# A chunk attention and ELU feed-forward kernel on one Trainium2 core: the head crossing moves from v's load into the scores, and sixteen warm-up products stand in place of thirteen

## The chip, the cores and the metric

The kernel runs on one core of one Trainium2 chip. The metric is the device time of one execution in microseconds; the kernel before takes 837.71 us (median of three, 837.11 to 837.82). The engines are TensorE (PE, with its weight loads as PEld), VectorE (DVE), ScalarE (ACT), GpSimd (POOL) and SyncE (SP). SP computes nothing here; it issues nearly all DMA requests.

## The reference

Chunked attention over 8 batches, 8 heads, 576 tokens and 64 columns a head, with chunks of 64 tokens that attend only to themselves, and then a feed-forward layer over the 4608 rows that result (512 columns):

```python
scores = scale * np.matmul(q_c, k_c.transpose(0, 1, 2, 4, 3))
scores = scores - np.max(scores, axis=-1, keepdims=True)
attn = np.exp(scores)
attn = attn / (np.sum(attn, axis=-1, keepdims=True) + 1e-09)
out = np.matmul(attn, v_c)
...
h = x @ w_in                     # 512 -> 2048; x is out with its heads side by side
g = np.where(h > 0.0, h, alpha * (np.exp(np.minimum(h, 0.0)) - 1.0))
return (g @ w_out).astype(np.float32)
```

`w_in` and `w_out` are double precision inputs of 512x2048 and 2048x512. All results are float32.

## The kernel before

**Work.** The 4608 rows are nine blocks of 512 tokens; a block is four tiles of 128 tokens, and a tile is two chunks. For every block the kernel computes `h` in 16 pieces of 128 hidden columns (`hidden`, PE products named `h`), the ELU of each piece (`elu`), and adds its product with `w_out` onto four output tiles (`second_next`, PE products named `o`). Each float32 operand is split into a high and a low part, and every product is three matmuls (`three`, L447). The last six blocks use a scheme with fewer multiplications whose operands are prepared during the earlier blocks; the change does not touch it.

**Weights.** They arrive as 64-bit words. A unit `u` (seventeen, 0 to 16) is one 128-column piece of `w_in` and the 128-row piece of `w_out` of the piece before, loaded by two requests of 512 KB into one of three staging buffers `st` (`load_unit`, L113 and L120). ACT rescales the high words (L134) and converts the low ones (L139); DVE clips (L156) and joins them in two steps (L163, L167); ACT rounds the result to the high part (L171) and DVE subtracts to get the low part (L177). A unit's buffer is free for the unit three later when its L167 is done.

**Attention of the first eight tiles** (`early_attention`). PE turns q and k (in the start with products of 64 columns, L288; later with transposes, L292), ACT copies them out of PSUM (L301 or L299), PE makes the scores (`score`, L263), DVE takes the maximum (L309), ACT the exponentials (L319, for most of the tiles head by head), DVE the normalisation (L332 to L334), PE turns the result (L339), ACT copies it (L344), PE multiplies with v (`multiply_v_crossed`, L255), and ACT copies the result into x (L438 or L433). Tiles 0 to 3 run in the opening part, called the start here; tiles 4 to 7 run inside the first feed-forward block, among its products. All later tiles use the class `Later`, with its own scores and its own product with v (L271), which read an uncrossed v.

**The crossing.** Scores go to two PSUM banks and two halves of the partitions. Before the change, for the second chunk the bank was swapped with the head's parity, so that after the turn (L339) the rows of a chunk's even and odd heads lie in opposite halves of the partitions for the two chunks. The rows of v must then lie in the matching halves, and `load_v_crossed` puts them there with four requests a tile, each 64 tokens of four heads (64 KB, L246).

**The order of the work** is written out by hand: strings of items name each step, and each engine executes its own instructions in the order of these strings. `START` holds the opening part (`w13` is thirteen transposes of the identity at L863, `q0` a load, a digit one step of that tile's attention, `u1` a unit's load, `r` and `d` one step of the weight preparation on ACT and on DVE, `g02` two filler products), `FIRST_BLOCK` the first block. The SP queue is in program order as well. Its requests signal over eight counters in turn, so a request also waits until the request eight before it (of SP and ACT together) has landed.

Of the kernel before, what the change touches and what calls it, by code (L numbers as in the profile page):

```python
# [21 lines left out]
def kernel(  # L22
# [27 lines left out]
    C = 64  # L50
# [186 lines left out]
    halves = [slice(i * C, (i + 1) * C) for i in range(2)]  # L237
    quarters = [(0, 0), (1, 1), (0, 1), (1, 0)]

    def load_v_crossed(n0: int, pool):  # L240

        dst = pool.tile([P, H, D], F32, name="v_sb").rearrange("p (c h) d -> p c h d", c=2)
        for c in range(2):
            b, s0 = divmod(n0 + c * C, S)
            for r in range(2):
                nc.sync.dma_start(  # L246
                    out=dst[halves[r], c],
                    in_=v[b, r ^ c::2, s0:s0 + C, :].rearrange("h t d -> t h d"))
        return dst

    def multiply_v_crossed(x_ps, v_sb, aT):
        for hp in range(NK):
            for c, j in quarters:
                rows = halves[j ^ c]
                nc.tensor.matmul(  # L255
                    x_ps[halves[j], c, hp, :], lhsT=v_sb[rows, c, hp, :],
                    rhs=aT[rows, hp, halves[c]], start=True, stop=True,
                )

    def score(scores, qT, kT, crossed=0):  # L260
        for hp in range(NK):
            for j, c in quarters:
                nc.tensor.matmul(  # L263
                    scores[halves[c], j ^ (c & crossed), hp, :], lhsT=qT[halves[j], hp, halves[c]],
                    rhs=kT[halves[j], hp, halves[c]], start=True, stop=True,
                )

# [11 lines left out]
    def early_attention(tt: int, q_sb, k_sb, get_v, kT, at, a_pool, get_banks, put, by_head: bool,  # L279
                        by_pair=None):  # L280


        both = get_banks()
        for i, src in enumerate((q_sb, k_sb)):
            for n in range(NK):
                if by_pair is not None:
                    for j, half in enumerate(halves):
                        nc.tensor.matmul(  # L288
                            both[half, i, n * P:(n + 1) * P], lhsT=src[:, j, n * D:(n + 1) * D], rhs=by_pair,
                            start=True, stop=True)  # L290
                else:
                    nc.tensor.transpose(  # L292
                        out=both[:, i, n * P:(n + 1) * P], in_=src[:, 2 * n:2 * n + 2, :],
                        identity=ident)
        yield
        qT = at.tile([P, NK, P], F32, name="qT")
        for i, to in enumerate((qT, kT)):
            if by_pair is None:
                nc.scalar.copy(out=to, in_=both[:, i, :].rearrange("p (h t) -> p h t", h=NK))  # L299
            else:  # L300
                nc.scalar.copy(  # L301
                    out=to.rearrange("p h (t u) -> p (h t) u", u=4),
                    in_=both[:, i, :].rearrange("p (u h) -> p h u", u=4))
        yield
        scores = first_halves(both)
        score(scores, qT, kT, 1)
        yield
        mx = sm.tile([P, 2, NK, 1], F32, name="mx")
        nc.vector.tensor_reduce(out=mx, in_=scores, axis=AX.X, op=ALU.max)  # L309
        a = a_pool.tile([P, H, C], F32, name="a")  # L310
        a_heads = a.rearrange("p (h j) t -> p j h t", j=2)
        z = sm.tile([P, 2, NK, 1], F32, name="z")
        if by_head:

            nc.vector.tensor_scalar_mul(mx, mx, -SCALE)
            yield
            for j in range(2):
                for h in range(NK):
                    nc.scalar.activation(  # L319
                        out=a_heads[:, j, h, :], in_=scores[:, j, h, :], func=AF.Exp, scale=SCALE,  # L320
                        bias=mx[:, j, h, :], accum_out=z[:, j, h, :],
                    )
            yield
        else:
            nc.vector.tensor_tensor(
                out=a_heads, in0=scores, in1=mx.broadcast_to([P, 2, NK, C]), op=ALU.subtract
            )
            yield
            nc.scalar.activation(out=a, in_=a, func=AF.Exp, scale=SCALE)
            yield  # L330
            nc.vector.tensor_reduce(out=z, in_=a_heads, axis=AX.X, op=ALU.add)
        nc.vector.tensor_scalar_add(z, z, 1e-9)  # L332
        nc.vector.reciprocal(z, z)
        nc.vector.tensor_tensor(  # L334
            out=a_heads, in0=a_heads, in1=z.broadcast_to([P, 2, NK, C]), op=ALU.mult
        )
        yield
        for hp in range(NK):
            nc.tensor.transpose(  # L339
                out=both[:, 0, hp * P:(hp + 1) * P], in_=a[:, 2 * hp:2 * hp + 2, :],  # L340
                identity=ident)
        yield
        aT = at.tile([P, NK, P], F32, name="qT")
        nc.scalar.copy(out=aT, in_=both[:, 0, :].rearrange("p (h t) -> p h t", h=NK))  # L344
        yield
        x_ps = first_halves(both)
        multiply_v_crossed(x_ps, get_v(), aT)
        yield
        put(tt, x_ps)
        yield  # L350
# [507 lines left out]
    def warm(n: int):  # L858
# [7 lines left out]

    BY_HEAD = (1, 3, 4, 5, 6, 7)
    START = (
        "q0 w13 k0 q1 k1 0 1 u0 0 q2 0 1 q3 r 1 r k2 0 2 1 d 0 0 d 1 1 k3 2 u1 3 3 g02 2 r d 3 u2 "
        "1 2 3 2 d v0 v1 0 g03 r v2 1 0 2 d v3 1 g21 3 2 2 r d 0 3 2 g32 d u3 s 3 0 3 s 2 1 3 g01 "  # L870
        "3 r d r"
    )
# [93 lines left out]
    with (  # L966
# [24 lines left out]
        for item in START.split():  # L991
            kind, n = item[0], item[1:]
            if kind == "w":
                warm(int(n))
            elif kind == "u":
                load_unit(int(n))
            elif kind in "qkv":
                src = {"q": q, "k": k, "v": v}[kind], f"{kind}_sb", int(n) * P, start
                loaded[kind, int(n)] = load_v_crossed(
                    int(n) * P, start) if kind == "v" else load_quads(  # L1000
                    *src, nc.scalar if item in ("k0", "k1") else nc.sync)
            elif kind == "r":
                next(preparation)
            elif kind == "d":
                next(merging)
            elif kind == "s":
                subtract_next()
            elif kind == "g":
                for _ in range(int(n[1:])):
                    nc.tensor.matmul(  # L1010
                        start_ps[int(n[0])][:, 1, NK * C:], lhsT=ident, rhs=two_idents,
                        start=True, stop=True)
            else:
                start_step(item)
# [20 lines left out]
    def early_tile(n: int):  # L1035

        n0 = n * P
        q_sb, k_sb = [load_heads(src, name, n0, io) for src, name in ((q, "q_sb"), (k, "k_sb"))]
        v_sb = load_v_crossed(n0, vio)
        return early_attention(  # L1040
            n % NTT, q_sb, k_sb, lambda: v_sb, k_turned, at, wi1,
            lambda: ps_early.tile([P, 2, DM], F32, name="ps_a"),
# [293 lines left out]
```

## Time and profile before

| | |
|---|---|
| median of three runs | 837.71 us |
| profiled execution, its own time | 838.7 us |
| its span, first to last instruction | 836.9 us |
| PE busy in it | 819.9 us (98%) |
| DVE, ACT, POOL busy | 620.4, 492.8, 186.7 us |
| mean granted TensorE clock | 0.998 |
| moved by DMA | 181.40 MB, mean 217 GB/s |
| v loads of L246 | 32 requests of 64 KB |

Times in the profile are microseconds from the start of the span. A row of the timeline gives start, duration, engine (SPq is SP's queue of instructions), line, operation, and in brackets how long the engine had been idle before and what ended that. A row of the windows view gives, for one stretch, the busy time and count of each engine, then the granted TensorE clock, the share of the DMA engines' time and GB/s. A matmul of float32 operands counts as two instructions in the profile (the 16 products of a tile with v are x32). Tile numbers are left out of the names; u3's request is the fourth L113 row, and so on.

### The profile page before, as it was taken

Reading aid. Unit: us, or ns where it says so; the run is one execution under the profiler, and the core shown is the slowest. Engines: PE = TensorE matmul, PEld = TensorE weight load, DVE = VectorE, ACT = ScalarE, POOL = GpSimd, SP = SyncE. Lnnn points to the kernel's source line nnn. Section 1 sums busy time; section 2 is a strip of 40 time slices with the busy share of each in tenths; the row PEclk is TensorE's granted clock in tenths of the full one; section 3 lists DMA queues with packets and bytes.
Section 4 is the critical chain, followed back from the end, with each engine's and each line's share of the span. In section 5 each row is a group of like instructions: output and inputs, shape, how many; then the busy total and the mean of one; then the engine's idle time right before and its main releaser. Section 6 shows DMA issues by size and latency. Waiting matters only on the chain.

```text
span 836.9 us, 15651 instructions
## 1 busy us (share of the span) xinstructions
PE 819.9 (98%) x5791; PEld 669.5 (80%) x5791; DVE 620.4 (74%) x945; ACT 492.8 (59%) x884; POOL 186.7 (22%) x196
## 2 busy tenths in 40 slices
PE   8879999999999999999999999999999999999997
PEld 7758777888888878788888888888888888888886
DVE  4978987777887688777877765877877547777744
ACT  5888996444554445666566435666556346776541
POOL 0000004444411211134323553324335000000000
PEclk9999999999999999999999999999999999999999
DMA  8756785788499997689999857699966457664666
GB/s 252 180 193 204 234 264 137 212 240 238 140 295 243 273 277 224 204 222 278 259 262 272 218 141 240 178 300 281 268 184 190 132 164 215 195 194 136 186 198 149
DMA packets 212379, 181.40 MB, mean 217 GB/s; under 512 B 74064, under 2 KB 190800, under 8 KB 212304
## 3 DMA queue, kind: packets, MB, share of 16 engines
q1 hardware_dynamic: 209648, 179.62, 76.6%
q10 hardware_dynamic: 2656, 0.79, 0.4%
q8 instruction: 46, 0.75, 0.4%
q14 instruction: 29, 0.24, 0.1%
HBM read 140.51 MB, written 42.99 MB: 219 GB/s over the span
## 4 chain that ended last, share of the span: by engine, by line
PE 84%; DVE 4%; ACT 4%; DMA 3%; issue 2%; SPq 2%; POOL 0%; DVEq 0%; ACTq 0%; POOLq 0%
PE o L447 42%; PE h L447 37%; PE ps_a L263 2%; DMA st<-in_moe_w_out_dram 2%; PE ps_a L271 2%; ACT a L319 1%; PE ps_a L288 1%; SPq L246 1%; PE h L464 1%; ACT st L134 1%; ACT st L139 1%; DMA q_sb<-in_q_dram 1%; SPq L198 0%; DMA wi_hi<-a_dram 0%; DVE xf L163 0%
## 5 line engine op out<-in xcount | busy, mean ns | idle before, releaser
L447 PE MATMUL o<-wo_hi,ghi 128*128 128x512 f32 x352 | 139.4, 396 | 0.0
L447 PE MATMUL o<-wo_hi,glo 128*128 128x512 f32 x352 | 138.2, 393 | 0.7 <-DVE glo L482 0.4
L447 PE MATMUL o<-wo_lo,ghi 128*128 128x512 f32 x352 | 137.9, 392 | 0.3 <-DVE wo_lo L177 0.3
L447 PE MATMUL h<-xhi,wi_hi 128*128 128x512 f32 x324 | 108.3, 395 | 1.4 <-ACT wi_hi L171 1.2
L447 PE MATMUL h<-xlo,wi_hi 128*128 128x512 f32 x324 | 106.8, 390 | 0.0
L703 POOL TENSOR_TENSOR glo<-e,ghi 128x512 fp32r<-128x512 f32 x32 | 41.3, 1291 | 172.8 <-ACT ghi L701 166.3
L447 PEld LDWEIGHTS o<-wo_hi,glo 128*128 128x128 f32 x352 | 66.5, 189 | 15.8 <-DVE glo L482 1.2
L447 PEld LDWEIGHTS o<-wo_hi,ghi 128*128 128x128 f32 x352 | 66.5, 189 | 14.1
L447 PEld LDWEIGHTS o<-wo_lo,ghi 128*128 128x128 f32 x352 | 66.5, 189 | 14.1 <-DVE wo_lo L177 0.6
L447 PE MATMUL h<-wi_lo,wi_hi 128*128 128x512 f32 x288 | 75.0, 396 | 0.0
L768 ACT COPY kept<-h 128x512 f32<-128x512 f32 x72 | 42.1, 585 | 55.4 <-PE h L447 55.4
L447 PEld LDWEIGHTS h<-xhi,wi_hi 128*128 128x128 f32 x324 | 60.6, 188 | 15.4 <-ACT wi_hi L171 1.6
L447 PE MATMUL h<-wo_lo,wi_hi 128*128 128x512 f32 x288 | 71.8, 389 | 0.0
L447 PE MATMUL o<-wo_hi,wo_lo 128*128 128x512 f32 x240 | 71.0, 390 | 0.0
L447 PEld LDWEIGHTS h<-xlo,wi_hi 128*128 128x128 f32 x324 | 60.8, 188 | 12.5 <-DVE xlo L681 0.3
L447 PE MATMUL h<-xhi,wi_lo 128*128 128x512 f32 x180 | 70.4, 391 | 0.2
L447 PEld LDWEIGHTS h<-wo_lo,wi_hi 128*128 128x128 f32 x288 | 54.1, 188 | 11.2
L693 ACT ACTIVATE e<-e 128x512 f32<-128x512 f32 x96 | 60.7, 633 | 3.1
L447 PEld LDWEIGHTS h<-wi_lo,wi_hi 128*128 128x128 f32 x288 | 52.9, 188 | 11.4 <-ACT c L768 0.2
L447 PE MATMUL o<-wo_lo 128*128 128x512 f32 x192 | 59.9, 389 | 0.0
L696 DVE SCALAR_TENSOR_TENSOR g_kept<-e,g_kept 128x512 f32<-128x512 f32 x48 | 33.6, 700 | 31.5 <-ACT e L693 31.5
L447 PEld LDWEIGHTS o<-wo_hi,wo_lo 128*128 128x128 f32 x240 | 45.0, 188 | 9.6 <-DVE kept L487 0.2
(174 smaller groups left out, 1582.2 us busy)
## 6 DMA issues: line engine op xcount, KB each, us to landing
wi_hi<-a_dram SPq DMA_DIRECT2D x168, 256.0 KB, 4.1
wo_lo<-lo_dram SPq DMA_DIRECT2D x36, 512.0 KB, 5.2
wo_lo<-b_dram SPq DMA_DIRECT2D x56, 256.0 KB, 3.0
kept<-in_q_dram SPq DMA_DIRECT2D x100, 128.0 KB, 4.2
kept<-in_k_dram SPq DMA_DIRECT2D x100, 128.0 KB, 4.3
st<-in_moe_w_in_dram SPq DMA_DIRECT2D x16, 512.0 KB, 5.0
st<-in_moe_w_out_dram SPq DMA_DIRECT2D x16, 512.0 KB, 5.6
a_dram<-kept SPq DMA_DIRECT2D x16, 512.0 KB, 3.8
```

The lines of the kernel that those rows point to most:

```text
L134: nc.scalar.mul(out=high.bitcast(F32), in_=high.bitcast(F32), mul=REBIAS)
L139: nc.scalar.activation(out=low, in_=top, func=AF.Copy, scale=2.0 ** -13, bias=2.0 ** -14 - 0.5)
L246: nc.sync.dma_start(out=dst[halves[r], c], in_=v[b, r ^ c::2, s0:s0 + C, :].rearrange("h t d -> t h d"))
L263: nc.tensor.matmul(scores[halves[c], j ^ (c & crossed), hp, :], lhsT=qT[halves[j], hp, halves[c]], rhs=kT[halves[j], hp, halves[c]], start ...
L271: nc.tensor.matmul(x_ps[halves[j], c, hp, :], lhsT=v_sb[halves[c], 2 * hp + j, :], rhs=aT[halves[c], :, j * NK + hp], start=True, stop=True,)
L288: nc.tensor.matmul(both[half, i, n * P:(n + 1) * P], lhsT=src[:, j, n * D:(n + 1) * D], rhs=by_pair, start=True, stop=True)
L319: nc.scalar.activation(out=a_heads[:, j, h, :], in_=scores[:, j, h, :], func=AF.Exp, scale=SCALE, bias=mx[:, j, h, :], accum_out=z[:, j, h ...
L447: nc.tensor.matmul(ps, lhsT=a, rhs=b, start=start, stop=stop, skip_group_check=onto)
L693: nc.scalar.activation(out=e, in_=e, func=AF.Exp, scale=-1.0)
L696: nc.vector.scalar_tensor_tensor(out=to, in0=e, scalar=-1.0, in1=c, op0=ALU.add, op1=ALU.max)
L703: engine.tensor_tensor(out=lo, in0=e, in1=hi.bitcast(F32), op=ALU.subtract)
L768: nc.scalar.copy(out=c21 if i == 4 else self.kept[i - 1], in_=x_ps)
```

## The change

Three edits. First, the scores of the early tiles are written by a new function, `score_crossed`: the bank is now the chunk, and the partition half is the chunk's index crossed with the head's parity. Second, v therefore needs no crossing: `load_v_crossed` is gone, and the early tiles load v with `load_heads`, as q and k and all later tiles do: one request of 128 tokens and eight heads (256 KB), or two where the tile lies across two batches (tile 4). Of the 32 requests 9 remain. `multiply_v_crossed` reads the rows of its own chunk. Third, `w16` stands for `w13`.

```diff
-    def load_v_crossed(n0: int, pool):
-        dst = pool.tile([P, H, D], F32, name="v_sb").rearrange("p (c h) d -> p c h d", c=2)
-        for c in range(2):
-            b, s0 = divmod(n0 + c * C, S)
-            for r in range(2):
-                nc.sync.dma_start(
-                    out=dst[halves[r], c],
-                    in_=v[b, r ^ c::2, s0:s0 + C, :].rearrange("h t d -> t h d"))
-        return dst
...
     def multiply_v_crossed(x_ps, v_sb, aT):
         for hp in range(NK):
             for c, j in quarters:
-                rows = halves[j ^ c]
                 nc.tensor.matmul(
-                    x_ps[halves[j], c, hp, :], lhsT=v_sb[rows, c, hp, :],
-                    rhs=aT[rows, hp, halves[c]], start=True, stop=True,
+                    x_ps[halves[j], c, hp, :], lhsT=v_sb[halves[c], 2 * hp + j, :],
+                    rhs=aT[halves[c], hp, halves[c ^ j]], start=True, stop=True,
                 )
-    def score(scores, qT, kT, crossed=0):
+    def score_crossed(scores, qT, kT):
+        for hp in range(NK):
+            for c, j in ((0, 0), (0, 1), (1, 0), (1, 1)):
+                nc.tensor.matmul(
+                    scores[halves[c ^ j], c, hp, :], lhsT=qT[halves[j], hp, halves[c]],
+                    rhs=kT[halves[j], hp, halves[c]], start=True, stop=True,
+                )
+
+    def score(scores, qT, kT):
         for hp in range(NK):
             for j, c in quarters:
                 nc.tensor.matmul(
-                    scores[halves[c], j ^ (c & crossed), hp, :], lhsT=qT[halves[j], hp, halves[c]],
+                    scores[halves[c], j, hp, :], lhsT=qT[halves[j], hp, halves[c]],
                     rhs=kT[halves[j], hp, halves[c]], start=True, stop=True,
                 )
...
-        "q0 w13 k0 q1 k1 0 1 u0 0 q2 0 1 q3 r 1 r k2 0 2 1 d 0 0 d 1 1 k3 2 u1 3 3 g02 2 r d 3 u2 "
+        "q0 w16 k0 q1 k1 0 1 u0 0 q2 0 1 q3 r 1 r k2 0 2 1 d 0 0 d 1 1 k3 2 u1 3 3 g02 2 r d 3 u2 "
         "1 2 3 2 d v0 v1 0 g03 r v2 1 0 2 d v3 1 g21 3 2 2 r d 0 3 2 g32 d u3 s 3 0 3 s 2 1 3 g01 "
...
-                loaded[kind, int(n)] = load_v_crossed(
-                    int(n) * P, start) if kind == "v" else load_quads(
+                loaded[kind, int(n)] = load_heads(*src) if kind == "v" else load_quads(
                     *src, nc.scalar if item in ("k0", "k1") else nc.sync)
...
-        q_sb, k_sb = [load_heads(src, name, n0, io) for src, name in ((q, "q_sb"), (k, "k_sb"))]
-        v_sb = load_v_crossed(n0, vio)
+        loaded = [load_heads(src, name, n0, pool)
+                  for src, name, pool in ((q, "q_sb", io), (k, "k_sb", io), (v, "v_sb", vio))]
+        q_sb, k_sb, v_sb = loaded
```

The steps on which the prediction turns are SP's requests from the third weight unit to the fifth, and PE's first instructions.

SP in the start and at the head of the first block (st is a weight unit's staging buffer: here the end of u2, then u3, then u4; q_sb, k_sb and v_sb a tile's inputs: v of tiles 0 to 3, then tiles 4 and 5), rows with - before and with + now:

```order
 L113 DMA st<-in_moe_w_in_dram 128x4x256
 L120 DMA st<-in_moe_w_out_dram 128x1024
-L246 DMA v_sb<-in_v_dram 64x4x64 x16
+L198 DMA v_sb<-in_v_dram 128x8x64 x4
 L113 DMA st<-in_moe_w_in_dram 128x4x256
 L120 DMA st<-in_moe_w_out_dram 128x1024
 L198 DMA q_sb<-in_q_dram 64x8x64 x2
 L198 DMA k_sb<-in_k_dram 64x8x64 x2
-L246 DMA v_sb<-in_v_dram 64x4x64 x4
+L198 DMA v_sb<-in_v_dram 64x8x64 x2
 L198 DMA q_sb<-in_q_dram 128x8x64
 L198 DMA k_sb<-in_k_dram 128x8x64
-L246 DMA v_sb<-in_v_dram 64x4x64 x4
+L198 DMA v_sb<-in_v_dram 128x8x64
 L113 DMA st<-in_moe_w_in_dram 128x4x256
 L120 DMA st<-in_moe_w_out_dram 128x1024
```

Nothing changed places; between u2 and u3 stand 4 requests in place of 16, and between u3 and u4 9 in place of 14.

PE at the very start (ident is the identity that the warm-up transposes, ps_a_109 the PSUM banks of tile 0, ps_a_147 those of tile 1, two_idents the matrix that turns q and k), before:

```order
L863 MATMUL ps_a_109<-ident_75 128x128 x13
L288 MATMUL ps_a_109<-two_idents_104,q_sb_107 64x128 x8
L288 MATMUL ps_a_109<-two_idents_104,k_sb_123 64x128 x8
L288 MATMUL ps_a_147<-two_idents_104,q_sb_125 64x128 x8
L288 MATMUL ps_a_147<-two_idents_104,k_sb_127 64x128 x8
```

and now (line numbers are four lower; tile 1's banks are ps_a_150):

```order
L859 MATMUL ps_a_109<-ident_75 128x128 x16
L284 MATMUL ps_a_109<-two_idents_104,q_sb_107 64x128 x8
L284 MATMUL ps_a_109<-two_idents_104,k_sb_126 64x128 x8
L284 MATMUL ps_a_150<-two_idents_104,q_sb_128 64x128 x8
L284 MATMUL ps_a_150<-two_idents_104,k_sb_130 64x128 x8
```

Three more transposes stand ahead of the first turn of q; everything behind them keeps its order.

More of the change, by code (lines that the diff above doesn't have):

```diff
@@ L305, in early_attention @@
         scores = first_halves(both)
-        score(scores, qT, kT, 1)
+        score_crossed(scores, qT, kT)
         yield
```

## The prediction, as put on record

> **What bounds the kernel now.** I read the windows view by stages first, then the waits in the stage that stands out, then the chain of waits back from them, then SP's timeline.
>
> ```profile
> 28.50:46.00 17.50, 16.87 (x134) 13.35 (x134) 12.59 (x17) 10.89 (x18) 0.00 (x0) 1.00 0.97 248
> 46.00:54.00 8.00, 3.79 (x17) 2.50 (x17) 6.70 (x12) 7.97 (x26) 0.00 (x0) 1.00 0.51 181
> 59.00:93.00 34.00, 34.00 (x246) 27.89 (x246) 30.88 (x43) 30.53 (x59) 0.00 (x0) 1.00 0.66 199
> 93.00:137.00 44.00, 42.34 (x306) 33.46 (x305) 38.46 (x58) 39.16 (x88) 0.00 (x0) 1.00 0.81 226
> 137.00:836.90 699.90, 694.48 (x4684) 568.26 (x4682) 511.43 (x780) 380.13 (x635) 185.98 (x190) 1.00 0.78 217
> ```
>
> The first busy column is PE, the third DVE, the fourth ACT. From 59 us on PE never rests for long, so what comes later moves as a block with the moment at which PE gets there. The hole is at 46 to 54 us: PE works 3.79 of 8 us while ACT works 7.97. ACT is not slow, it is late: in the stage before it worked 10.89 of 17.5 us. The waits of 28 to 70 us (total, times, longest) say on what:
>
> ```profile
> ACT st L134 <- DMA st<-in_moe_w_out_dram: 6.2, 2, 5.5
> ```
>
> and the chain of waits says why that DMA was late:
>
> ```profile
> 35.23 0.94 SPq L246
> ...
> 38.25 0.54 SPq L113
> ...
> 38.84 6.68 DMA st<-in_moe_w_out_dram
> ```
>
> The chain runs along SP's queue, not through a freed buffer. SP issued u4 at 38.25 and 38.84, its last piece landed at 45.52, and ACT had stood idle for 5.5 us. SP's timeline up to there, and DVE's L167, which frees the buffers that u3 and u4 take (those of u0 and u1):
>
> ```profile
> 9.52 15.67 SPq L246 DMA_DIRECT2D v_sb<-in_v_dram  x16
> 25.32 1.93 SPq L113 DMA_DIRECT2D st<-in_moe_w_in_dram  x1
> ...
> 30.52 3.39 SPq L246 DMA_DIRECT2D v_sb<-in_v_dram  x4
> 33.95 0.60 SPq L198 DMA_DIRECT2D q_sb<-in_q_dram  x1
> ```
> ```profile
> 18.10 0.68 DVE L167 SCALAR_TENSOR_TENSOR xf<-st,xf 128x512 uint32<-128x512 uint32 x1
> 24.63 1.22 DVE L167 SCALAR_TENSOR_TENSOR xf<-st,xf 128x1024 uint32<-128x1024 uint32 x1
> ```
>
> u3 could have gone at 18.8 and went at 25.3; u4 could have gone at 25.9 and went at 38.3. The v requests, four a tile, fill SP's queue in between (0.98 each in the first sixteen, where several also wait for the request eight before them; 0.73 to 0.85 later).
>
> **The late load (first and main term).** A request for 256 KB of the same form costs SP what one for 64 KB does (33.95: 0.60 us). Four v requests from 9.52 end near 12, so SP then waits for u0's buffer: u3 goes at 18.8 in place of 25.3. Behind it nine requests in place of fourteen, 0.6 each, and u1's buffer: u4 could be issued at about 26. What limits it then is the transfer. In the window 27 to 40 us, where most packets are 256 bytes, the DMA row and its rate are
>
> ```profile
> DMA  0005589999999999999997725348999999874579
> GB/s 11 10 19 126 151 280 375 375 457 422 416 417 293 277 268 219 214 206 208 205 197 132 156 54 136 70 94 201 277 265 284 287 224 221 139 166 96 129 115 138
> ```
>
> so full engines move about 207 GB/s in such packets and some 365 (estimate, from 293 to 457 in the same row) in the weights' longer ones. The last of u2 landed 9.6 us after its issue at 8.76 (the DMA view of 9 to 26 us), at 18.4:
>
> ```profile
> st<-in_moe_w_out_dram SPq DMA_DIRECT2D x1, 512.0 KB, 9.6
> ```
>
> Up to u4 there follow ten loads of 256 KB (v of four tiles, q, k, v of two; 2.62 MB, 12.7 us) and u3 and u4 (2.10 MB, 5.8 us): u4 lands at about 36.9 in place of 45.5. The rule that a request waits for the eighth before it binds early (u4's first waits for q of tile 4), but these land in the order of the same queue, so it adds no more.
>
> Who wants u4 when? ACT, when it has rounded ghi:
>
> ```profile
> 32.13 1.17 ACT L134 ACTIVATE st<-st 128x1024 f32<-128x1024 f32 x1 [0.72 <-DMA st<-in_moe_w_out_dram]
> 39.53 0.62 ACT L479 CAST ghi<-e 128x512 fp32r<-128x512 f32 x1 [0.38 <-DVE e L474]
> 42.44 0.69 PE L263 MATMUL ps_a<-k_turned,qT 64*64 64x64 f32 x32
> ```
>
> That ends at 40.15, or 39.4 since u3's earlier landing also removes the 0.72 at 32.13. So ACT takes u4 at 39.4 in place of 45.6, 6.2 earlier, 2.5 us after it landed. Next late is DVE: its maximum needs the scores that PE ends at 43.13, so from there DVE moves up about 5.1, ACT with it. PE meets this:
>
> ```profile
> 47.27 0.50 PE L447 MATMUL h<-xhi,wi_hi 128*128 128x512 f32 x1 [1.18 <-ACT wi_hi L171]
> ...
> 53.62 0.63 PE L339 MATMUL ps_a<-ident,a 128*128 128x128 f32 x4 [2.95 <-DVE a L334]
> 54.00 0.47 PE L447 MATMUL o<-wo_hi,ghi 128*128 128x512 f32 x1
> ...
> 59.03 0.69 PE L255 MATMUL ps_a<-qT,v_sb 64*64 64x64 f32 x32
> ```
> ```profile
> 62.67 2.72 PE o L447 x12
> ```
> ```profile
> 55.00:57.00 2.00, 2.00 (x6) 1.54 (x6) 1.84 (x4) 1.97 (x4) 0.00 (x0) 0.50 0.90 340
> ```
>
> Both waits go: PE finishes h at 49.5, and the attention result that L339 waits for (ready at 53.47) is there at 48.4. That is 1.18 + 2.95 = 4.13. The idle time also cost clock: at 55 to 57 the granted clock is 0.50, and the twelve products from 54.00 to 59.03 take 5.03 where the chain shows 2.72 for twelve. Without the hole that goes too: 2.31. Together PE gains 6.4, 1.3 more than DVE. Does DVE hold it back then?
>
> ```profile
> 60.61 0.68 DVE L482 TENSOR_TENSOR glo<-e,ghi 128x512 fp32r<-128x512 f32 x1
> ```
> ```profile
> 62.96 0.39 PE L447 MATMUL o<-wo_hi,glo 128*128 128x512 f32 x1
> ```
> ```profile
> 68.15 0.60 ACT L471 ACTIVATE e<-h 128x512 f32<-128x512 f32 x1 [1.53 <-PE h L447]
> ```
>
> PE takes glo 1.67 after it is ready, enough for the 1.3; at 68.15 ACT itself waits 1.53 for PE, and there the others catch up. I take **6.4**. Bounds: 4.1 if the clock's share is lost again to a wait, and 8.1 if all of PE's idle 1.66 in 93 to 137 went as well (tile 7's v request frees SP there, too).
>
> **The warm-up (second term).**
>
> ```profile
> 1.36 3.04 PE L863 MATMUL ps_a<-ident 128*128 128x128 f32 x13 [1.36 <-POOL ident masks.py:199]
> 5.10 1.98 PE L288 MATMUL ps_a<-two_idents,q_sb 128*64 128x128 f32 x16 [0.70 <-DMA q_sb<-in_q_dram]
> 6.83 1.95 PE L288 MATMUL ps_a<-two_idents,k_sb 128*64 128x128 f32 x16
> 8.54 1.95 PE L288 MATMUL ps_a<-two_idents,q_sb 128*64 128x128 f32 x16
> 10.24 1.19 PE L288 MATMUL ps_a<-two_idents,k_sb 128*64 128x128 f32 x16
> ```
> ```profile
> 15.89 1.04 PE L288 MATMUL ps_a<-two_idents,k_sb 128*64 128x128 f32 x16
> ```
> ```profile
> 11.47 0.58 ACT L301 COPY qT<-ps_a 128x512 f32<-128x512 f32 x1 [1.58 <-PE ps_a L288]
> ```
>
> Three transposes more take 0.64 (3.04 for 13, less the last one's tail) and end at about 5.04, before q's arrival lets PE start at 5.10: they delay nothing, and should q come sooner, at most 0.6. They fill the 0.70. A group of sixteen takes 1.95 until about 10.4 and 1.04 later: half rate. If a stretch without the hole is what grants the clock, full rate comes one stretch sooner. The half-rate period at 55 us lasted 3.4 (0.94 of the clock at 54 to 55, 0.85 at 58 to 59), so I put it at 7.1 in place of 10.5. Then the second group saves about 0.76 (five sixths of 0.91), the third 0.91, the fourth 0.15: **1.8**. ACT waits for the fourth group at 11.47, and from there to u3 it is the bound of the start (its later gaps are under 0.3), so the 1.8 passes to the first block, whose loads are now no longer set by SP. Bounds: 0, and 2.7 (three groups saved whole).
>
> The Trainium skill (TensorE: Matmul & The Clock Gate, "What's actually happening") gives a free-running window of 3413 ns, which agrees with the 3.4 here; by it the 1.8 would vary from run to run.
>
> **At nothing.** The new scores use the same quarters of PE in the same order. The products with v alternate halves of the rows, as the later tiles' do:
>
> ```profile
> L271 PE MATMUL ps_a<-turned,v_sb x896: 217/218/267, 154.4 to 630.2; 64*64 64x64 f32 x180
> L255 PE MATMUL ps_a<-qT,v_sb x256: 217/218/268, 22.6 to 133.6; 64*64 64x64 f32 x128
> ```
>
> 218 ns both; unhidden it would be a few ns for each of 256. v now arrives in one piece behind u2, by 18.4 plus 1.3 a tile, so 19.7 to 23.5; the first product with v comes at 22.6 (20.8 with the warm-up's gain) and takes tile 1's, there at 21. A wait of 0.2 lies on PE, which waits for ACT anyway.
>
> **The sum.** 6.4 + 1.8 = 8.2. The profiled execution took 838.7 (span 836.9 and 1.8 around it), 1.0 over the median of 837.71. It becomes 830.5, and the median **829.5 us**.
>
> **The rivals.** *The warm-up buys nothing* (chance 0.30). The added instructions are transposes; if the grant counts only products, those run from 5.10 to 7.10 in the stretch concerned, as before, and full rate comes at 10.5 again. For it: the stretch from 3.7 to 7.1 was four fifths full of transposes and products before, and did not suffice. Against: no row shows that transposes count less. The first block still gains 6.4: 831.3. The Trainium skill (TensorE: Matmul & The Clock Gate, "Part 4: PE-mode transpose") says that transposes do not count as busy in the same way; no row here shows it.
>
> *DVE and ACT become the bound* (0.12). At 59 to 93 they work 30.9 and 30.5 of 34 us, so little is left to catch up with; if PE waits for glo, only the idle 4.1 is won, with 1.8: 831.8. Against it is the slack of 1.67.
>
> *The u4 wait only changes its cause* (0.04), another request being late: about 837.7. Against it are 2.5 us of room.
>
> *Long requests in small packets clog the queue* (0.04): slower. The same ten loads stand whole ahead of u4. While v trickled in they moved slowly:
>
> ```profile
> DMA packets 2650, 0.67 MB, mean 84 GB/s; under 512 B 2648, under 2 KB 2648, under 8 KB 2648
> ```
>
> (18 to 26 us). At 84 GB/s, 2.62 MB take 31.2, and u4 lands at 55.4, 9.9 late: 847.6. It decides below 123 GB/s (2.62 MB in the 21.3 us left up to 45.5). Against: there the queue was empty between requests, and full it did 207.
>
> **How the numbers follow.** My forecast has 0.50, the rivals 0.30, 0.12, 0.04, 0.04. The range 827.0 to 833.6 reaches from both terms at their upper bounds (837.7 - 8.1 - 2.7 = 826.9) to PE's idle time alone (837.7 - 4.1); the two rivals that save less lie inside it. A change under 0.2% (1.7 us), about the scatter of such measurements, counts as the same: 0.04 from the third rival; slower 0.04; faster 0.92.
>
> **What would show it.** Right: u3 issued near 17 to 19, u4 landed before 38, no idle of ACT over 1 us at L134 for u4, no idle of PE of 2.95 at L339, no half clock near 55, L288's second group shorter than 1.95, and PE's window after 137 as before but 8 us earlier. Wrong: a landing of u4 after 40, groups of 1.95 until 10 us, or new waits of PE on DVE between 54 and 93.

## The result

The changed kernel takes **829.60 us** (median of four runs, 828.93 to 829.85), beside 837.77 for the kernel before (four runs, 837.11 to 838.25). The ratio is 0.9902, 95% interval 0.9885 to 0.9919: 8.2 us less. The profiled execution took 829.4 (span 827.6), 9.3 less than the one of before.

Line numbers behind 240 are lower by 4 to 12 in the changed kernel: v is loaded at L198 like q and k, the scores are L251, the product with v L243, DVE's maximum L305, the turn of the result L335, the three matmuls of a product L443, the first turns L284, the warm-up L859.

The windows view of the changed kernel, cut at about the same places of the program as before (what PE did from 47.27 to 59.03 us now lies from 44.06 to 50.25; columns: PE, PEld, DVE, ACT, POOL, then clock, DMA share, GB/s):

```profile
26.60:43.00 16.40, 15.73 (x130) 12.67 (x131) 15.36 (x23) 15.55 (x28) 0.00 (x0) 1.00 0.91 256
43.00:50.00 7.00, 7.00 (x34) 5.57 (x32) 6.83 (x11) 6.97 (x21) 0.00 (x0) 1.00 0.45 162
50.00:84.00 34.00, 34.00 (x246) 27.70 (x245) 32.05 (x44) 32.03 (x61) 0.00 (x0) 1.00 0.65 198
84.00:128.00 44.00, 42.62 (x309) 34.10 (x308) 39.21 (x59) 39.33 (x88) 0.00 (x0) 1.00 0.78 229
128.00:827.60 699.60, 694.15 (x4682) 568.00 (x4680) 509.81 (x779) 380.04 (x635) 185.96 (x190) 1.00 0.78 217
```

The hole is gone: where PE worked 3.79 of 8 us before, it works 7.00 of 7. ACT, which stood idle for 6.6 of the 17.5 us ahead of the hole, now works 15.55 of 16.4 there. The last stage is as long as before. PE's timeline at the place of the hole:

```profile
44.06 0.39 PE L443 MATMUL h<-xhi,wi_hi 128*128 128x512 f32 x1
...
46.78 0.60 PE L335 MATMUL ps_a<-ident,a 128*128 128x128 f32 x4
47.13 0.48 PE L443 MATMUL o<-wo_hi,ghi 128*128 128x512 f32 x1
...
50.25 0.69 PE L243 MATMUL ps_a<-qT,v_sb 64*64 64x64 f32 x32
```

No bracket stands behind any of these rows: PE waits for nothing. SP's timeline shows what made the room:

```profile
10.20 8.54 SPq L198 DMA_DIRECT2D v_sb<-in_v_dram  x4
18.87 1.15 SPq L113 DMA_DIRECT2D st<-in_moe_w_in_dram  x1
...
29.68 1.19 SPq L198 DMA_DIRECT2D v_sb<-in_v_dram  x1
30.98 0.84 SPq L113 DMA_DIRECT2D st<-in_moe_w_in_dram  x1
31.86 0.50 SPq L120 DMA_DIRECT2D st<-in_moe_w_out_dram  x1
```

u3 goes at 18.87 (before: 25.32), u4 at 30.98 (38.25). ACT's row for u4:

```profile
37.91 1.15 ACT L134 ACTIVATE st<-st 128x1024 f32<-128x1024 f32 x1 [0.29 <-DMA st<-in_moe_w_out_dram]
```

It waits 0.29 us where it waited 5.5. And the first turns of q and k, after three more warm-up transposes:

```profile
1.36 3.67 PE L859 MATMUL ps_a<-ident 128*128 128x128 f32 x16 [1.36 <-POOL ident masks.py:199]
5.02 1.97 PE L284 MATMUL ps_a<-two_idents,q_sb 128*64 128x128 f32 x16
6.75 1.11 PE L284 MATMUL ps_a<-two_idents,k_sb 128*64 128x128 f32 x16
7.68 1.06 PE L284 MATMUL ps_a<-two_idents,q_sb 128*64 128x128 f32 x16
8.55 1.06 PE L284 MATMUL ps_a<-two_idents,k_sb 128*64 128x128 f32 x16
...
28.59 1.18 PE L460 MATMUL h<-xhi,wi_hi 128*128 128x512 f32 x4
```

The second group is fast already; the records of the granted clock give full speed from 6.85 us on, before from 10.51.

**Where the time came from**, by PE's timelines of the two profiled executions (start of the same instruction, before and after; wi_hi and wi_lo are the high and low part of a unit's piece of `w_in`, wo_hi and wo_lo of `w_out`):

| PE's instruction | before | after | gained so far | by |
|---|---|---|---|---|
| first product of the first block | 30.46 | 28.59 | 1.87 | the start |
| first product of the h piece behind the first wait | 47.27 | 44.06 | 3.21 | the wait of 1.18 for wi_hi |
| its third product | 48.08 | 44.51 | 3.57 | a short wait for wi_lo |
| L339, now L335 | 53.62 | 46.78 | 6.84 | the wait of 2.95 |
| tile 4's product with v | 59.03 | 50.25 | 8.78 | the half clock (1.6) and a short wait for wo_lo (0.3) |
| end of the span | 836.9 | 827.6 | 9.3 | small waits from 95 to 128 us |

The 1.6 and 0.3 of the fifth row are parted by a run below (the filled wait), in which the wait for wo_lo stands without the half clock.

### The profile page after: what moved, and what is told of

Read it like the earlier page. It is cut to its first block, busy times and chain, and to the rows that moved or that the text cites. A ratio compares the mean times of both kernels' runs of the same rounds, so it can differ in the third digit from the quotient of the medians.

```text
span 827.6 us, 15634 instructions
## 1 busy us (share of the span) xinstructions
PE 816.1 (99%) x5794; PEld 667.6 (81%) x5794; DVE 619.1 (75%) x945; ACT 493.0 (60%) x884; POOL 186.7 (23%) x196
## 4 chain that ended last, share of the span: by engine, by line
PE 87%; DMA 4%; ACT 4%; DVE 3%; issue 2%; SPq 1%; POOL 0%; POOLq 0%; ACTq 0%; DVEq 0%
PE o L443 42%; PE h L443 39%; PE ps_a L259 2%; PE ps_a L267 2%; PE h L460 1%; DMA kept<-in_k_dram 1%; ACT a L315 1%; DMA st<-in_moe_w_out_dram 1%; DMA kept<-in_q_dram 1%; DMA b_dram<-lo_dram 1%; PE ps_a L284 1%; PE ps_a L859 0%; ACT st L139 0%; DVE qT L365 0%; DVE k_turned L365 0%
## 5 line engine op out<-in xcount | busy, mean ns | idle before, releaser
L443 PE MATMUL o<-wo_hi,ghi 128*128 128x512 f32 x352 | 138.8, 394 | 0.0
L443 PE MATMUL o<-wo_hi,glo 128*128 128x512 f32 x352 | 137.5, 391 | 0.7 <-DVE glo L478 0.5
L443 PE MATMUL o<-wo_lo,ghi 128*128 128x512 f32 x352 | 137.2, 390 | 0.0
L443 PE MATMUL h<-xhi,wi_hi 128*128 128x512 f32 x324 | 108.2, 394 | 0.2 <-ACT kept L764 0.2
L443 PE MATMUL h<-xlo,wi_hi 128*128 128x512 f32 x324 | 106.8, 390 | 0.0
L443 PEld LDWEIGHTS o<-wo_hi,glo 128*128 128x128 f32 x352 | 66.1, 188 | 15.6 <-DVE glo L478 1.2
L443 PEld LDWEIGHTS o<-wo_hi,ghi 128*128 128x128 f32 x352 | 66.1, 188 | 14.1
L443 PEld LDWEIGHTS o<-wo_lo,ghi 128*128 128x128 f32 x352 | 66.1, 188 | 13.6 <-DVE wo_lo L177 0.2
L443 PE MATMUL h<-wi_lo,wi_hi 128*128 128x512 f32 x288 | 75.1, 396 | 0.0
L443 PEld LDWEIGHTS h<-xhi,wi_hi 128*128 128x128 f32 x324 | 60.7, 188 | 13.9 <-ACT kept L764 1.1
L443 PE MATMUL h<-wo_lo,wi_hi 128*128 128x512 f32 x288 | 71.8, 389 | 0.0
L443 PE MATMUL o<-wo_hi,wo_lo 128*128 128x512 f32 x240 | 70.9, 390 | 0.0
L443 PEld LDWEIGHTS h<-xlo,wi_hi 128*128 128x128 f32 x324 | 60.8, 188 | 12.5 <-DVE xlo L677 0.3
L443 PE MATMUL h<-xhi,wi_lo 128*128 128x512 f32 x180 | 70.2, 390 | 0.0
L443 PEld LDWEIGHTS h<-wo_lo,wi_hi 128*128 128x128 f32 x288 | 54.1, 188 | 11.2
L443 PEld LDWEIGHTS h<-wi_lo,wi_hi 128*128 128x128 f32 x288 | 52.9, 188 | 11.4 <-ACT c L764 0.2
L443 PE MATMUL o<-wo_lo 128*128 128x512 f32 x192 | 59.9, 389 | 0.0
L443 PEld LDWEIGHTS o<-wo_hi,wo_lo 128*128 128x128 f32 x240 | 45.1, 188 | 9.5 <-DVE kept L483 0.2
```

Of the source, the lines that this page charges most:

```text
L443: nc.tensor.matmul(ps, lhsT=a, rhs=b, start=start, stop=stop, skip_group_check=onto)
```

## The experiments

The runs were made in three further comparisons, in which the kernel before had medians of 838.47 (23 runs), 838.72 (7) and 839.08 us (17), single runs from 836.63 to 840.72. The ratios below are each to the runs of before in the same comparison. This table gathers what the profiles of all kernels show, one execution of each; "first product" is that of the first block on PE's timeline, "rest" is the span less that, "full from" and "half windows" (but for the last 3 us of the span) are from the records of the granted clock.

| kernel | v requests a tile (start, block) | warm-up | full from | half windows at | first product | rest | median us |
|---|---|---|---|---|---|---|---|
| before | 4, 4 | 13 | 10.51 | 54.88 | 30.46 | 806.4 | 837.8 to 839.1 |
| sixteen alone | 4, 4 | 16 | 5.63 | 22.70, 50.00, 56.83 | 29.96 | 809.8 | 838.27 |
| filled wait | 4, 4 | 13 | 10.44 | none | 30.44 | 807.4 | 837.13 |
| four, all tiles | 4, 4 | 16 | 5.94 | 53.73 | 28.92 | 805.8 | 837.79 |
| four, start | 4, 1 | 16 | 6.16 | 50.53 | 28.33 | 805.3 | 834.93 |
| four whole, start | 4, 1 | 16 | 4.67 | none | 28.52 | 803.0 | 833.71 |
| four, block | 1, 4 | 16 | 4.44 | none | 28.36 | 802.0 | 831.43 |
| two, start | 2, 1 | 16 | 7.35 | none | 28.97 | 799.2 | 829.59 |
| **the change** | 1, 1 | 16 | 6.85 | none | 28.59 | 799.0 | 829.60 |
| u4 first | 1, 1 | 16 | 6.42 | none | 28.52 | 799.5 | 829.12 |
| thirteen | 1, 1 | 13 | 7.13 | none | 28.73 | 798.9 | 829.46 |
| one | 1, 1 | 1 | 9.63 | none | 30.02 | 798.9 | 830.88 |
| earlier warm-up | 1, 1 | 20 products | 6.48 | none | 31.06 | 799.2 | 831.27 |
| sixty | 1, 1 | 60 | 5.93 | none | 32.97 | 798.9 | 833.74 (one run) |

Two things are read from it at once. In the kernels with the change's load form, the rest is 798.9 to 799.5 whatever the start does, so the start passes on to the end one for one. And the rest grows with the number of v requests, to 805 to 810.

### Is it the load's form or the new scores?

The change, with v in four uncrossed requests a tile:

```diff
-                loaded[kind, int(n)] = load_heads(*src) if kind == "v" else load_quads(
+                loaded[kind, int(n)] = load_four(*src) if kind == "v" else load_quads(
...
+        parts = dst.rearrange("p (g r) d -> p r g d", r=2)
+        for c in range(2):
+            b, s0 = divmod(n0 + c * C, S)
+            for r in range(2):
+                nc.sync.dma_start(
+                    out=parts[c * C:(c + 1) * C, r],
+                    in_=src[b, r::2, s0:s0 + C, :].rearrange("h s d -> s h d"))
```

(and the same in `early_tile`).

> The change with its crossed scores, but v of the early tiles loaded in four requests a tile again (64 tokens of every other head, uncrossed). Theory (the number of requests fills SP's queue, the crossing itself costs nothing): u3 issued near 25, u4 landed near 45.5, ACT's wait of 5 us at L134 and PE's of 2.9 at L339 back, 837 us. Rival (the new scores or the plain product with v bring the gain): 829.6.

837.79 us, ratio 0.9993 (0.9981 to 1.0005): no difference from before can be told. ACT's row for u4 in that kernel:

```profile
43.84 1.12 ACT L134 ACTIVATE st<-st 128x1024 f32<-128x1024 f32 x1 [4.39 <-DMA st<-in_moe_w_out_dram]
```

The whole gain is in the load's form. The crossed scores, the plain product with v and three more transposes, all of which this kernel has, give nothing that can be measured.

### Which tiles' requests?

The same four requests for tiles 0 to 3 alone (first), and for tiles 4 to 7 alone (second).

> The change, with four requests a tile for tiles 0 to 3 alone. Theory (the sixteen requests of the start make most of the delay: in the kernel before they held SP for 15.7 us, the four of tile 4 for 3.4 and the four of tile 5 for about 3): u3 issued near 25, u4 near 33 to 36, landed at 40 to 43 in place of 37.8; ACT wants it at 37.9 and PE has about 1.5 of room, so 831 to 834 us. Rival (u3's place doesn't count, since u4's buffer and the transfers of tiles 4 and 5 set it): 829.6 to 830.2.

> The change, with four requests a tile for tiles 4 to 7 alone. Theory (u3 goes as early as in the change, and behind it SP has eight requests of 0.6 us in place of three that took 2.3, 0.6 and 1.2): u4 issued at 31 to 34, landed at 38 to 41; 829.6 to 831.5 us. Rival (the requests of tiles 4 and 5 alone made u4 late, as they stand just ahead of it): 836 to 838.

834.93 us, ratio 0.9959 (0.9947 to 0.9971), and 831.43, ratio 0.9912 (0.9895 to 0.9928). Of the 8.2 us between the change and four requests everywhere, by the medians the start's sixteen account for 5.3 and the block's for 1.8, which leaves 1.0 to both together. The parting is good to a microsecond or so: by the ratios, each to its own comparison's runs of before, it is 4.8 and 0.8 of 7.6. The first was worse than expected, since the lateness was enough for the half clock. The waits of 28 to 70 us in the first:

```profile
ACT st L134 <- DMA st<-in_moe_w_out_dram: 4.7, 2, 3.3
...
PE ps_a L346 <- DVE a L341: 3.0, 1, 3.0
```

and in the second:

```profile
ACT st L134 <- DMA st<-in_moe_w_out_dram: 2.5, 1, 2.5
...
PE ps_a L346 <- DVE a L341: 1.3, 1, 1.3
```

ACT's wait passes to PE less 0.3 to 1.2; PE then waited 3.0 in the one, and its clock was halved at 50.53, and 1.3 in the other, where the clock held.

### Is it the number of requests or their shape?

For tiles 0 to 3, two requests a tile of 128 tokens and four heads; then four of 128 tokens and two heads, in place of four of 64 tokens and four heads (the diff is of the first; the second steps through the heads by two):

```diff
+        for h0 in (0, 4):
+            for p0, b, s0, n in pieces_of(n0, 1):
+                nc.sync.dma_start(
+                    out=dst[p0:p0 + n, h0:h0 + 4],
+                    in_=src[b, h0:h0 + 4, s0:s0 + n, :].rearrange("h s d -> s h d"))
```

> The change, with v of tiles 0 to 3 in two requests a tile, each of 128 tokens and four heads (128 KB). Theory (what held SP before was the limit of eight requests in flight and 0.6 a request, not the bytes): eight requests, the limit binds at most for the last ones (u2 lands at 18.0 and stands nine ahead of the last), u3 issued at 18.8 to 20, 829.6 to 830.0 us. Rival (what holds SP is the queue's room for packets, the same in any number of requests): u3 at 18.8 and 829.6 exactly as the change; only the four-request kernels, whose requests write half the partitions, differ.

> The change, with v of tiles 0 to 3 in four requests a tile as in the run with four in the start alone, but each of all 128 tokens and two heads in place of 64 tokens and four heads: the same 16 requests of 64 KB and the same packets. Theory (the number of requests is what holds SP: 0.6 each and eight in flight): u3 issued near 25 again, 834.9 us as in that run. Rival (requests on half of the partitions move slowly, and that is what held SP): u3 near 19, 829.6 us.

829.59 us, ratio 0.9892 (0.9877 to 0.9906), and 833.71, ratio 0.9933 (0.9917 to 0.9948; single runs from 830.8 to 834.45). SP's timelines of the kernels with two, with four whole, and with four half requests in the start, from about the landing of u2 on:

```profile
17.78 2.90 SPq L207 DMA_DIRECT2D v_sb<-in_v_dram  x3
20.81 0.42 SPq L113 DMA_DIRECT2D st<-in_moe_w_in_dram  x1
```
```profile
19.65 4.47 SPq L207 DMA_DIRECT2D v_sb<-in_v_dram  x9
24.25 0.38 SPq L113 DMA_DIRECT2D st<-in_moe_w_in_dram  x1
```
```profile
18.74 5.87 SPq L209 DMA_DIRECT2D v_sb<-in_v_dram  x9
24.74 0.82 SPq L113 DMA_DIRECT2D st<-in_moe_w_in_dram  x1
```

The number decides, mostly. In every kernel SP stands at the v requests until about the landing of u2: with four a tile because the eighth v request must wait for it (it is eight behind u2's second half), with one or two because the requests themselves are held (8.54 us for the change's four; by what is not shown). What differs is how many requests remain after that: none in the change, about two in the second form, nine with four a tile, at 0.50 each where they write 128 partitions (4.47 for nine) and 0.65 where they write 64 (5.87 for nine). So the shape has a share as well, 0.15 a request, which neither expectation had (and u3's 20.81 lies just behind the 18.8 to 20 that the first one gave); the median of the whole form is 1.2 below that of the half one.

### Does the wait cost clock beside itself?

The kernel before, with one piece's products made twice, so that PE is busy while it waits:

```diff
         if f:
-            for kt in range(NK):
-                three(h, hi[:, kt, :], lo[:, kt, :], xhi[:, kt, :], xlo[:, kt, :],
-                      kt == 0, kt == NK - 1)
+            for again in range(2 if len(hiddens) == 4 else 1):
+                for kt in range(NK):
+                    three(h, hi[:, kt, :], lo[:, kt, :], xhi[:, kt, :], xlo[:, kt, :],
+                          kt == 0, kt == NK - 1)
```

> The kernel before, with the twelve products of one h piece (those from 47.27 to 50.67 us) made a second time into the same bank, so that PE works through 2.8 of the 2.95 us that it waited at L339. Nothing else waits for the repetition, and u4 is as late as before. Theory (the idle time also cost clock, 2.3 us in the prediction): no half clock near 50 to 58, the twelve products behind L339 take 2.7 in place of 5.0, and the time is 2.3 less than before, about 836.2 us, with less scatter. Rival (the loss was the wait alone): the same as before, or up to 0.3 more for the repetition.

837.13 us, ratio 0.9981 (0.9971 to 0.9992): 1.6 less by the ratio, 0.7 to 2.4 by its interval. PE's timeline there:

```profile
54.73 0.63 PE L339 MATMUL ps_a<-ident,a 128*128 128x128 f32 x4 [0.26 <-DVE a L334]
55.12 0.47 PE L447 MATMUL o<-wo_hi,ghi 128*128 128x512 f32 x1
...
58.57 0.69 PE L255 MATMUL ps_a<-qT,v_sb 64*64 64x64 f32 x32
```

No half clock, and the twelve products take 3.45 in place of 5.03: 1.6 in the profile too. The other runs agree: the mean granted clock of the twelve is 0.998 to 1.000, that of the seventeen of before in the same comparison 0.995 to 0.998. Useless work in a wait paid for itself, so the clock's loss is real and apart from the wait. It is smaller than the 2.3 of the theory, which set the 5.03 beside 2.72 for twelve products without any wait: the 3.45 still hold a wait of 0.26 for wo_lo, and even the change's twelve, without it, take 3.12. The scatter did not shrink, though (836.06 to 839.64), and the profiled execution is one of the slowest: it lost what it had won in waits at 37 us and from 114 to 128, where ACT waited 3.0 for another unit's load.

### Was the last 0.29 of u4's wait on the path?

```diff
-        "H r s e d L4 d L5 e e s e d u4 H 4 e 4 e e r d e H e s r d P 4 s 4 u5 e 4 d e P d 4 e s "
+        "H r s e d L4 d e e s e d u4 L5 H 4 e 4 e e r d e H e s r d P 4 s 4 u5 e 4 d e P d 4 e s "
```

> The change with the three loads of tile 5 moved behind u4. Theory (ACT's wait of 0.29 for u4 lies off the path: DVE waits 0.83 for PE's scores right after it): u4 issued near 27, landed near 33, ACT's wait gone, PE's times from 46 us on the same within 0.3, 829.6 us within 0.4. Rival (the 0.29 is on the path): 829.3. Second rival (u4's later landing was where the change's remaining loss lay): 828.8 or less.

829.12 us, ratio 0.9886 (0.9872 to 0.9901); single runs from 828.54 to 829.76 overlap those of the change. ACT's row for u4 is free of its wait,

```profile
37.47 1.16 ACT L134 ACTIVATE st<-st 128x1024 f32<-128x1024 f32 x1
```

and the product at 50.87 us of the change starts at 50.87 here as well. The wait was off the path.

### What are the warm-up transposes worth?

The change with thirteen and with one, and the kernel before with sixteen (`w13`, `w1` and `w16` in `START`).

> The change, but with thirteen warm-up transposes as before. Theory (the transposes count toward the clock's grant, and the start's gain passes to the end): full clock near 10.5 us again, the first block's first product near 30.4 in place of 28.6, and 831.4 us, 1.8 more than the change. Rival (the clock's window runs freely, so thirteen are often enough): no fixed place of the transition, and a median between 829.6 and 830.5. Second rival (the gain of the start is absorbed later by a wait): transition at 10.5, but 829.6.

> The change with one warm-up transpose in place of sixteen. Theory (the start's clock passes to the end one for one; without the warm-up the grant comes at the end of the first window that lies behind q's arrival, between 7.9 and 11.3 us): the fourth group of L284 ends at 10.1 to 12 in place of 9.3 to 9.9, and the time is 1.4 more, about 831.0 us, scattered from 830.2 to 832. Rival (the start is absorbed, or the warm-up buys nothing): 829.6.

> The kernel before with sixteen warm-up transposes as the only edit. Theory (u4 is late because of SP's queue, which the warm-up doesn't touch, so the start's gain is swallowed by the wait for u4): first products 1.8 earlier, u4 landing at 45.5 as before, 837.5 us, at most 0.5 less than before. Rival (the two terms add): 836.0, 1.8 less than before.

Thirteen: 829.46 us (828.43 to 831.25), ratio 0.9894 (0.9880 to 0.9909): the same median as with sixteen, with more scatter. One: 830.88 us (830.56 to 831.4), ratio 0.9905 (0.9891 to 0.9918); by the medians 1.3 to 1.8 over the change, thirteen, two in the start and u4 first, and the table shows it where it was expected, in a first product at 30.02. Sixteen alone: 838.27 us, ratio 1.0004 (0.9991 to 1.0017), as the theory had it; but since sixteen are worth no more than thirteen in the change either, the time of this run tells nothing of a gain that is swallowed. Its profile shows one way in which a gain goes, in this execution at least:

```profile
20.52 0.72 PE L255 MATMUL ps_a<-qT,v_sb 64*64 64x64 f32 x6 [0.91 <-DMA v_sb<-in_v_dram]
21.86 0.68 PE L255 MATMUL ps_a<-qT,v_sb 64*64 64x64 f32 x26 [0.61 <-DMA v_sb<-in_v_dram]
```

PE came to the first product with v, tile 1's, sooner than v: the last of that tile's requests, the eighth, had waited for u2's landing (19.47), went at 19.49 and landed at 21.82. After these two waits the clock was halved at 22.70, and the first block began at 29.96, where the other seven profiles with sixteen have 28.3 to 29.0.

Why thirteen were as good is seen in PE's timeline of that run:

```profile
1.35 3.04 PE L859 MATMUL ps_a<-ident 128*128 128x128 f32 x13 [1.35 <-POOL ident masks.py:199]
4.93 1.97 PE L284 MATMUL ps_a<-two_idents,q_sb 128*64 128x128 f32 x16 [0.54 <-DMA q_sb<-in_q_dram]
6.67 1.29 PE L284 MATMUL ps_a<-two_idents,k_sb 128*64 128x128 f32 x16
```

q arrived 0.17 sooner than in the profile of before, the hole was 0.54 in place of 0.70, and full clock came at 7.13. Three profiles with thirteen show it at 10.51, 10.44 and 7.13; eight with sixteen all between 4.44 and 7.35.

### Do transposes count toward the clock?

The change with sixty transposes (`w60`).

> Sixty warm-up transposes, so that PE does nothing but transposes from 1.4 to about 10 us. Theory (transposes count toward the grant): full clock by 7 to 8.5 us, amid the transposes; the later of them take 270 ns to finish in place of 421, and the warm-up ends near 11. Rival (only products count, as Part 4 of the Trainium skill's page TensorE: Matmul & The Clock Gate says): half rate throughout the transposes, which end near 14.5, and full clock only 3.4 to 6.8 us after the first product.

```profile
1.36 8.98 PE L859 MATMUL ps_a<-ident 128*128 128x128 f32 x60 [1.36 <-POOL ident masks.py:199]
10.27 1.09 PE L284 MATMUL ps_a<-two_idents,q_sb 128*64 128x128 f32 x16
```

Full clock came at 5.93, when PE had done nothing but transposes. At the cold rate of 0.213 (0.64 for three, in the prediction) sixty take 12.8; they took 8.98, and the first turn behind them takes 1.09, the figure of full clock. In two profiles with sixteen, too, full clock came before any other product had run: at 4.44 (four, block) and 4.67 (four whole, start), ahead of q's first turn at 5.61 and 5.11. They count. The Trainium skill says the opposite (TensorE: Matmul & The Clock Gate, "Part 4: PE-mode transpose"); the measurement decides.

### An attempt to be faster than the change

The order with u4 first, and a warm-up that need not wait for the identity (`w20`, moved ahead of `q0`):

```diff
+        blank = start.tile([P, P], F32, name="blank", bufs=1)
+        nc.vector.memset(blank, 0.0)
         make_identity(nc, ident)
...
-            nc.tensor.transpose(out=warm_ps[:, i % 4, :], in_=ident, identity=ident)
+            nc.tensor.matmul(warm_ps[:, i % 4, :], lhsT=blank, rhs=blank, start=True, stop=True)
```

> The change with tile 5's loads behind u4 as in the run before, and with twenty products of a zeroed tile as the warm-up in place of sixteen transposes of the identity: PE need not wait for the identity (1.36 us) and starts near 0.5. Theory (the grant comes at the end of the first free-running window of 3.4 us that is over four fifths busy, so it moves from 4.1 to 7.5 us to 3.3 to 6.7, and each of these 0.85 us that lies behind q's arrival saves half of it): 829.1 less 0.2 to 0.4, so 828.8 us. Rival (zeros or the earlier start count for nothing): 829.1 to 829.6.

831.27 us, ratio 0.9910 (0.9896 to 0.9923): slower than the change, by an error of sizing.

```profile
1.05 7.30 PE L859 MATMUL ps_a<-blank 128*128 128x128 f32 x40 [1.05 <-DVE blank L967]
8.29 1.09 PE L284 MATMUL ps_a<-two_idents,q_sb 128*64 128x128 f32 x16
```

A float32 product of this size is two instructions, so that twenty are forty, and each product took 0.36 at a mixed clock where I had put 0.21 as for a transpose. q was turned 3.3 us later than in the change, of which 2.5 reached the first block (first product 31.06). PE also started only 0.31 sooner, at 1.05. Whether an earlier start helps is left open. No version tried is faster than the change by more than the measurement tells.

## Why the prediction was right, and where it was not

**What bounds the kernel** was right: u4's lateness through SP's queue, which is ACT's wait, then PE's, then clock. Four requests for all tiles bring all of it back (837.79), four for a part of them a part of it, and no kernel that keeps the change's load form shows it.

**The first term (6.4)** had the right mechanism and was too small. In the profiled pair it is 7.4 (9.3 less 1.87 of the start). The two idle times gave 4.5 (1.34 and 3.12 by PE's starts, for 1.18 and 2.95). The half clock gave 1.6 (5.03 less the 3.45 of the filled wait), for 2.31: the 2.72 that the twelve products were set beside are those of twelve without any wait, and the 5.03 held a wait for wo_lo as well. Three pieces were not in the sum by name: that wait for wo_lo (0.3, the 3.45 less 3.12 now), the one for wi_lo (0.5), and 0.5 of small waits behind 93 us, which the prediction had only as an upper bound. In the three profiles with four requests for all tiles and no filling the rest runs from 805.8 to 809.8, so against 799 the term is 6.7 to 10.8 from execution to execution. It goes with the half windows behind the first product: one, one and, in the longest, two.

**Its steps on SP.** "Four v requests from 9.52 end near 12" was wrong: the four took 8.54, single ones up to 3.66, though others of the same size took 0.44 and 0.62. So u3's issue at 18.87, where 18.8 was predicted, is luck. The prediction had SP wait for u0's buffer until then, but in the changed kernel the earlier start freed it at 16.94:

```profile
16.26 0.68 DVE L167 SCALAR_TENSOR_TENSOR xf<-st,xf 128x512 uint32<-128x512 uint32 x1
```

What SP waited for was its own v requests, for 1.9 us more. What these 1.9 us cost is not shown; u3 later still, at 20.81 in the kernel with two requests, cost nothing that can be measured. u4 was issued at 30.98, not 26, and landed at 37.8, just ahead of ACT's row, against 36.9 predicted from the rates: the sum of the transfers gave the landing within 1 us although the issue was 5 us off. The room of 2.5 us was not there: ACT was ready at 37.62, 1.8 sooner than I had put it because I left the warm-up's own gain out of ACT's demand, and the landing was 0.9 later. It cost nothing, as DVE then waits for PE:

```profile
41.34 0.69 DVE L305 TENSOR_REDUCE mx<-ps_a 128x8 f32<-128x512 f32 x1 [0.83 <-PE ps_a L251]
```

**The second term (1.8)** is right for the pair of executions it was worked out from (1.87) and wrong for the median. With thirteen, the clock of the profiled execution before came one window late; in other executions it does not, and in the median the three added transposes give nothing (829.46 beside 829.60). The mistake was to take one execution's phase for the kernel's. The sentence that by a free-running window (the Trainium skill, TensorE: Matmul & The Clock Gate, "What's actually happening") the 1.8 would vary from run to run was the better guide, and belonged in the sum.

**So 829.5 came out right partly by two errors that cancel.** The load form alone, without the warm-up, gives 8.9 us by the ratio (7.6 to 10.1), where I had 6.4; the three transposes give none, where I had 1.8. The three runs of before that the forecast starts from (837.71) also lie below the medians of the larger sets (838.47 to 839.08).

**At nothing** held: the product with v is unchanged, and the first of them goes at 20.7 with no wait for v.

```profile
L243 PE MATMUL ps_a<-qT,v_sb x256: 218/218/267, 20.7 to 124.2; 64*64 64x64 f32 x128
```

**The rivals.** *The warm-up buys nothing* is true of the median, but not by its mechanism, since transposes count; and its 831.3 fails because the first term is larger. *DVE and ACT become the bound* fell: PE works 34.00 of 34.00 us behind the hole, with DVE at 32.05 and ACT at 32.03, so they came near. *The u4 wait changes its cause* and *long requests clog the queue* fell with 0.29 us of wait; the long requests did hold SP (8.54 us for the four), but not long enough to make u4 late.

## What to carry to other kernels

When a load is late though its buffer was free, look at the requests ahead of it on the queue and count them, not their bytes: a limit on requests in flight turns a late landing into a late issue for all that stands behind it, and each request left over then costs half a microsecond or more. A wait of TensorE should be priced with the clock that it loses (here 1.6 us for a window of 3.41 us at half rate), and a gain in clock that hangs on where a window falls should be priced over several executions, not from one. Repeating useful or useless products in a wait that can't be removed can pay.

## What the runs showed of the hardware

**The clock's windows.** In every profile the changes of the granted clock lie a whole number of 3.413 us apart (before: 10.51, 54.88 = 13 windows later, 58.29 = one more), at another phase in each execution. PE's busy time in the window that ended at the first grant, or did not bring it, and in those that lost the clock or kept it, sorts without overlap. Before the first grant (the clock column reads 1.00 there, since its records begin with the grant; the rate is seen in the groups of L288): the kernel before, not granted; thirteen, granted; four in all tiles, granted:

```profile
3.68:7.10 3.42, 2.72 (x24) 2.34 (x24) 0.00 (x0) 0.00 (x0) 0.00 (x0) 1.00 0.99 317
```
```profile
3.72:7.13 3.41, 2.87 (x26) 2.50 (x26) 0.00 (x0) 0.00 (x0) 0.00 (x0) 1.00 1.08 363
```
```profile
2.53:5.94 3.41, 2.85 (x16) 2.48 (x16) 0.00 (x0) 0.90 (x1) 0.00 (x0) 1.00 0.94 307
```

So between 2.72 and 2.85 of 3.41 us busy (80 and 84%) brings full clock. Sixteen alone lost it behind both of these, four whole kept it behind this one:

```profile
19.28:22.70 3.42, 1.80 (x35) 1.16 (x34) 3.28 (x7) 3.42 (x19) 0.00 (x0) 1.00 0.37 81
46.59:50.00 3.41, 1.82 (x8) 0.88 (x7) 1.90 (x3) 3.03 (x5) 0.00 (x0) 1.00 1.05 380
```
```profile
45.63:49.04 3.41, 1.92 (x9) 1.26 (x7) 3.01 (x5) 3.41 (x18) 0.00 (x0) 1.00 0.05 19
```

Somewhere between 1.82 and 1.91 of 3.41 (53 and 56%; another window of that kernel was kept at 1.91) is the point below which one window loses it. PE need not be idle for a whole window: two waits of 0.91 and 0.61, or one of 1.50, were enough in the two windows lost. The busy times rest on modelled ends, so the points are these profiles', not exact. By these figures sixteen should be the safer number, since they take 0.64 off the hole ahead of q, which with thirteen (0.54 to 0.77 us) puts a window that holds it right at the upper point. The times show no more of it than the wider scatter of thirteen (five runs, 828.43 to 831.25).

**One request can hold SP for several microseconds.** The v requests of the changed kernel (all of them, in the view by tile; minimum, median and longest):

```profile
L198 SPq DMA_DIRECT2D v_sb<-in_v_dram x40: 372/556/3657, 10.2 to 590.0; - x40
```

The same 256 KB take SP 0.4 to 0.6 us as a rule and up to 3.7. The two longest began at 10.93 and 14.12, while u2 was still on its way (landed at 18.02); what held them is not shown. So the duration of a request on SP is no constant to multiply with.
